# The last batch of an attention-and-Hyena kernel: output projection over four banks in the order in which its operand comes, own output buffers, final products on VectorE

## The chip, the cores and the metric

One core of a Trainium2 chip. The metric is the time of one execution in device microseconds (us), less is better. The kernel before takes 407.2 us (median of 4 runs, 406.5 to 408.2).

A second measure does much of the work here, because the change touches the last tenth of the program alone: the **stretch from batch 7's first eo to the end**, read from one trace as the span minus the start of the first of the two records that make tile eo (the even and odd halves of a batch, made in front of x2p) of the last batch. On every engine the changed kernel's order of instructions is that of the kernel before until this record. "After eo" below always means this.

## The reference

```python
def _attn_ref(q, k, v, omega):            # q, k, v: 8 batches, 8 heads, 576 rows, 64 columns
    ...                                   # random features cos, sin; kv = phi(k)^T v; num / den
x = attn_out.transpose(0, 2, 1, 3).reshape(8, 576, 512)
proj = x @ w_proj                         # 512 -> 3 x 512
x1, x2, x3 = proj[..., :512], proj[..., 512:1024], proj[..., 1024:]
x2_conv = irfft(rfft(x2, axis=1) * H)     # along the 576 rows
y = x1 * x2_conv * x3
out = y @ w_out                           # fp32, 8 x 576 x 512
```

## The kernel before

The batches go round a software pipeline: while one batch's attention part runs, the part after it (`hyena`) of the batch before runs beside it. In the last round there is only `hyena` of batch 7. A batch's `hyena` makes x2p (x2 before the transform), the spectrum (yp, ym, tc, yg), the gates (xg, w: x1 times x3), the inverse (xc, od, cv), the product yT, and the projection op with its copies o and their stores.

```python
        self.pt = self.pool("pt", 2, space=psum)          # two tiles of two PSUM banks, used by attention
        self.ps = self.pool("ps", 4, space=psum)          # four tiles of one bank, for everything else
...
    def inverse(self, b, dc):                              # 128 of the 512 columns
        ...                                                # xc on TensorE, od on ScalarE, cv on VectorE (bufs=2)
        nc.gpsimd.tensor_tensor(
            self.yT[b][:, dc], self.w.pop((b, dc)).rearrange("p a s -> p (a s)"),
            cv.rearrange("p c z i -> p (c z i)"), ALU.mult,
        )

    def project_out(self, b):
        nc, mo, yT = self.nc, self.mo, self.yT[b]
        every4 = self.out[b].rearrange("(i r) d -> r i d", r=4)
        for c in range(NC):                                # five chunks of 128, 128, 128, 128, 64 rows
            n = CH[c]
            ps = self.bank([128, DM], f"op{b}_{c}")
            _mm_acc(nc, ps[:n], [(yT[:, kc, 128 * c : 128 * c + n], self.wo[kc]) for kc in range(4)])
            o = mo.tile([128, DM], FP32, name=f"o{b}_{c}", tag="osb", bufs=2)
            nc.scalar.mul(o[:n], ps[:n], 1.0 / YS)
            for blk, i, m, at in _pieces(128 * c, n, QB):  # one or two stores a chunk, eight in all
                nc.sync.dma_start(every4[BLOCKS[blk], i : i + m], o[at : at + m])
...
        for b in range(B + 1):
            for hp in range(4):
                if b < B:
                    self.pair(b, hp)                       # attention
                ...
                if b:
                    self.hyena(b - 1, hp)
...
    def hyena(self, b, part):
        if part == 0:
            self.x2_project(b)
            self.gates(b, 0)
        elif part == 1:
            self.spectrum(b)
            self.gates(b, 1)
        elif part == 2:
            self.gates(b, 2)
            self.inverse(b, 0)
            self.gates(b, 3)
            self.inverse(b, 1)
        else:
            self.inverse(b, 2)
            self.inverse(b, 3)
            self.project_out(b)
```

Of the kernel before, what the change touches and what calls it, by code (L numbers as in the profile page):

```python
# [9 lines left out]
FP32 = mybir.dt.float32  # L10
# [5 lines left out]
ALU = mybir.AluOpType  # L16

B = 8
# [3 lines left out]
DM = H * D  # L22
NC = 5
CH = [128, 128, 128, 128, 64]
# [3 lines left out]
YS = 4096.0  # L28
# [6 lines left out]
QB = S // 4  # L35
EB = QB // 2
BLOCKS = [0, 1, 2, 3]
# [53 lines left out]
def _pieces(lo, n, block):  # L91

    at = lo
    while at < lo + n:
        k, i = divmod(at, block)
        m = min(block - i, lo + n - at)
        yield k, i, m, at - lo
        at += m
# [10 lines left out]
def _mm_acc(nc, outap, pairs):  # L109
    n = len(pairs)  # L110
    for i, (l, r) in enumerate(pairs):
        nc.tensor.matmul(outap, l, r, start=(i == 0), stop=(i == n - 1))  # L112
# [6 lines left out]
class _Program:  # L119
# [461 lines left out]
    def inverse(self, b, dc):  # L581
        nc, mo = self.nc, self.mo
        cols = slice(128 * dc, 128 * (dc + 1))
        if dc == 0:
            self.yT[b] = mo.tile([128, 4, S], FP16, name=f"yT{b}", tag="yT", bufs=1)
        half = []
        for g in (1, 0):
            ps = self.bank([128, HS], f"xc{b}_{dc}_{g}")
            ls = [self.yg[g][:, 0, cols], self.yg[g][:, 1, cols], self.ymix[:, cols]]
            _mm_acc(nc, ps, [(l, self.inv[:, 3 * g + i]) for i, l in enumerate(ls)])  # L590
            half.append(ps)
        od = mo.tile([128, HS], FP32, name=f"od{b}_{dc}", tag="od", bufs=2)
        nc.scalar.copy(od, half[0])
        cv = mo.tile([128, 4, 2, EB], FP32, name=f"cv{b}_{dc}", tag="cv", bufs=2)
        ev, ov = (x.rearrange("p (c i) -> p c i", i=EB) for x in (half[1], od))
        nc.vector.tensor_tensor(cv[:, :, 0], ev, ov, ALU.add)
        nc.vector.tensor_tensor(cv[:, :, 1], ev, ov, ALU.subtract)  # L597
        nc.gpsimd.tensor_tensor(  # L598
            self.yT[b][:, dc], self.w.pop((b, dc)).rearrange("p a s -> p (a s)"),
            cv.rearrange("p c z i -> p (c z i)"), ALU.mult,  # L600
        )

    def project_out(self, b):
        nc, mo, yT = self.nc, self.mo, self.yT[b]
        every4 = self.out[b].rearrange("(i r) d -> r i d", r=4)
        for c in range(NC):
            n = CH[c]
            ps = self.bank([128, DM], f"op{b}_{c}")
            _mm_acc(nc, ps[:n], [(yT[:, kc, 128 * c : 128 * c + n], self.wo[kc]) for kc in range(4)])
            o = mo.tile([128, DM], FP32, name=f"o{b}_{c}", tag="osb", bufs=2)  # L610
            nc.scalar.mul(o[:n], ps[:n], 1.0 / YS)  # L611
            for blk, i, m, at in _pieces(128 * c, n, QB):
                nc.sync.dma_start(every4[BLOCKS[blk], i : i + m], o[at : at + m])

    def run(self):
        for name in ("vf", "kT", "qT", "kf", "kft", "qf", "kvz", "xsd", "xT", "w", "yT", "marks", "pool_marks",
                     "first", "h"):
            setattr(self, name, {})
        self.pools()
        self.omega_load()  # L620
        self.first_loads()
        self.buffers()
        self.front(0, 0)
        self.second_loads()
        self.v_loads(1)
        self.weights()
        self.v_split_tails(0)
        for b in range(B + 1):
            for hp in range(4):
                if b < B:  # L630
                    self.pair(b, hp)
                if b == hp == 1:
                    self.filter_spectrum(1)
                    self.filter_spectrum(2)
                if b:
                    self.hyena(b - 1, hp)
                if b < 2:
                    self.opening(b, hp)

    def opening(self, b, hp):  # L640

        at = 4 * b + hp
        if at == 2:
            self.first_k_tails(1)
            self.first_k(1, 0)
        elif at == 3:
            self.first_k(1, 1)
            self.first_q(1, 3, 3)
        elif at == 4:
            with self.tc.issue_after(self.pool_marks["k", 1, 1].ins):  # L650
                self.loads(2)
            self.fold_filter()
            self.first_k(1, 2)
            self.first_q(1, 6, 2)
            self.filter_spectrum(0)
        elif at == 5:
            self.first_k(1, 3)
            self.out_weights()
# [27 lines left out]
# [12 lines that stand above are left out]
        else:  # L698
            self.inverse(b, 2)
            self.inverse(b, 3)  # L700
            self.project_out(b)



@with_exitstack
# [44 lines left out]
```

## Time and profile before

| | before |
|---|---|
| median of 4 runs, us | 407.17 |
| span of the profiled run, us | 404.8 |
| first eo of batch 7 to the end, us | 42.82 |
| yp starts, after eo | 14.40 |
| last yT ends, after eo | 31.47 |
| first copy o starts, after eo | 31.96 |
| last store issued, after eo | 39.38 |

The lines behind it are in the prediction: the chain of work that ended last, and the timeline, in which the brackets give the idle time of the engine before the instruction and what ended it.

### The profile page before, as it was taken

Reading aid. Unit: us, or ns where it says so; the run is one execution under the profiler, and the core shown is the slowest. Engines: PE = TensorE matmul, PEld = TensorE weight load, DVE = VectorE, ACT = ScalarE, POOL = GpSimd, SP = SyncE. Lnnn points to the kernel's source line nnn. Section 1 sums busy time; section 2 is a strip of 40 time slices with the busy share of each in tenths; the row PEclk is TensorE's granted clock in tenths of the full one; section 3 lists DMA queues with packets and bytes.
Section 4 is the critical chain, followed back from the end, with each engine's and each line's share of the span. In section 5 each row is a group of like instructions: output and inputs, shape, how many; then the busy total and the mean of one; then the engine's idle time right before and its main releaser. Section 6 shows DMA issues by size and latency. Waiting matters only on the chain.

```text
span 404.8 us, 9053 instructions
## 1 busy us (share of the span) xinstructions
PE 333.9 (82%) x3714; PEld 220.8 (55%) x3714; DVE 268.8 (66%) x489; ACT 246.1 (61%) x332; POOL 240.0 (59%) x222
## 2 busy tenths in 40 slices
PE   3786888987779978898789888997989888987981
PEld 2565645565336754566455744674557545663650
DVE  4686644777637887597839784978578784871740
ACT  1777766476675477746883679458764787124332
POOL 0654588669733977297827883597537672532450
PEclk9869589999889999999999999999999999999997
DMA  7999899636931593049613972369400021002103
GB/s 183 302 293 245 197 165 189 134 105 75 180 112 62 88 195 115 15 112 150 157 54 105 126 174 66 105 76 161 118 3 0 2 84 36 2 2 87 30 2 117
DMA packets 71465, 44.76 MB, mean 111 GB/s; under 512 B 38656, under 2 KB 64896, under 8 KB 71424
## 3 DMA queue, kind: packets, MB, share of 16 engines
q1 hardware_dynamic: 53712, 34.12, 33.2%
q0 software_dynamic: 17712, 10.06, 18.4%
q8 instruction: 29, 0.48, 0.5%
q14 instruction: 12, 0.10, 0.1%
HBM read 36.83 MB, written 16.52 MB: 132 GB/s over the span
## 4 chain that ended last, share of the span: by engine, by line
PE 34%; DVE 24%; POOL 17%; ACT 13%; issue 6%; DMA 4%; SPq 2%; POOLq 0%; ACTq 0%; DVEq 0%
PE xg L112 9%; PE kv L495 8%; DVE tc L559 7%; POOL yT L598 6%; ACT qf L479 5%; POOL angq L421 4%; DVE angk L420 4%; PE op L112 4%; PE nd L512 3%; PE xc L112 3%; DMA out_dram<-o 3%; PE x2p L112 3%; DVE angq L420 3%; ACT kf L458 3%; DVE xsd L518 2%
## 5 line engine op out<-in xcount | busy, mean ns | idle before, releaser
L458 ACT ACTIVATE kf<-angk 128x2048 f16<-128x2048 int16 x32 | 61.1, 1909 | 42.1 <-PE nd L512 18.0
L479 ACT ACTIVATE qf<-angq 128x1728 f16<-128x1728 int16 (+1 forms) x48 | 70.5, 1480 | 22.9 <-POOL angq L421 16.6
L112 PE MATMUL xg<-xT,wp 128*128 128x288 f16 x512 | 71.9, 286 | 1.3 <-ACT x L548 0.4
L420 DVE TENSOR_SCALAR angq<-thq 128x864 int32<-128x864 f32 (+1 forms) x48 | 45.7, 954 | 27.6 <-ACT qf L479 20.8
L112 PEld LDWEIGHTS <-wp 128*128 128x128 f16 x512 | 48.6, 97 | 20.8 <-issue 4.6
L401 POOL TENSOR_TENSOR vl<-vf,vh 128x512 f16<-128x512 f32 x32 | 39.1, 1221 | 31.6 <-ACT vh L400 31.2
L421 POOL TENSOR_SCALAR angk<-angk 128x1024 int32<-128x1024 int32 x32 | 33.5, 1047 | 34.7 <-DVE angk L420 33.7
L598 POOL TENSOR_TENSOR yT<-w,cv 128x576 f16<-128x576 f32 x32 | 45.1, 1430 | 14.5 <-DVE cv L597 7.4
L112 PE MATMUL op<-wo,yT 128*128 128x512 f16 (+1 forms) x160 | 42.7, 393 | 11.7 <-POOL yT L598 11.3
L421 POOL TENSOR_SCALAR angq<-angq 128x864 int32<-128x864 int32 (+1 forms) x48 | 43.1, 898 | 15.4 <-DVE angq L420 14.9
L578 DVE TENSOR_TENSOR w<-xg,w 128x288 f32<-128x288 f32 x64 | 27.4, 452 | 37.0 <-ACT w L576 19.3
L495 PEld LDWEIGHTS <-kf 128*128 128x128 f16 x1024 | 44.4, 101 | 13.1 <-issue 11.1
L560 POOL TENSOR_TENSOR yg<-tc,tc 128x1024 fp32r<-128x1024 f32 x16 | 37.4, 2359 | 23.6 <-DVE tc L559 22.1
L420 DVE TENSOR_SCALAR angk<-thk 128x1024 int32<-128x1024 f32 x32 | 39.0, 1219 | 16.7 <-PE thk L452 7.1
L576 ACT ACTIVATE w<-xg 128x288 f32<-128x288 f32 x64 | 24.5, 407 | 36.5 <-PE xg L112 35.8
L495 PE MATMUL kv<-vh,kf 128*128 128x65 f16 x512 | 39.1, 200 | 5.4 <-ACT w L576 4.7
L112 PE MATMUL x2p<-wp,eo 128*128 128x512 f16 x160 | 39.4, 403 | 2.8 <-DVE xsd L518 2.1
L559 DVE TENSOR_TENSOR tc<-yp,h 128x1024 f32<-128x1024 f32 x32 | 36.9, 1215 | 2.3 <-ACT vh L400 2.2
L495 PE MATMUL kv<-vl,kf 128*128 128x64 f16 x512 | 38.0, 198 | 0.2 <-POOL vl L401 0.2
L512 PE MATMUL nd<-kvz,qf 128*128 128x65 f16 x640 | 27.3, 197 | 10.3 <-DVE kvz L500 6.4
L611 ACT ACTIVATE o<-op 128x512 f32<-128x512 f32 (+1 forms) x40 | 22.9, 592 | 18.9 <-PE op L112 10.0
L512 PEld LDWEIGHTS <-qf 128*128 128x128 f16 x640 | 24.8, 99 | 16.2 <-issue 13.0
(84 smaller groups left out, 604.7 us busy)
## 6 DMA issues: line engine op xcount, KB each, us to landing
vf<-in_v_dram SPq DMA_DIRECT2D x7, 1024.0 KB, 5.4
qD<-in_q_dram POOLq DMA_DIRECT2D x6, 576.0 KB, 7.4
kD<-in_k_dram POOLq DMA_DIRECT2D x6, 512.0 KB, 5.8
ka<-in_k_dram SPq DMA_DIRECT2D x4, 512.0 KB, 11.4
out_dram<-o SPq DMA_DIRECT2D x8, 256.0 KB, 2.6
out_dram<-o SPq DMA_DIRECT2D x8, 224.0 KB
wp<-in_moe_w_proj_dram POOLq DMA_DIRECT2D x1, 1536.0 KB, 15.7
out_dram<-o SPq DMA_DIRECT2D x8, 192.0 KB
```

Of the source, the lines that this page charges most:

```text
L112: nc.tensor.matmul(outap, l, r, start=(i == 0), stop=(i == n - 1))
L401: nc.gpsimd.tensor_tensor(self.vl[hp], vp, vh, ALU.subtract)
L420: self.nc.vector.tensor_scalar(into, th, TO_PHASE, None, ALU.mult)
L421: self.pool_mark = self.nc.gpsimd.tensor_scalar(t[:, 1], t[:, 0], 1.0, TURN / 4, ALU.mult, ALU.add)
L458: self.marks["k", b, hp] = nc.scalar.activation(kf.rearrange("p t r a c m -> p t (r a c m)"), ang, AF.Sin, scale=TO_ANGLE)
L479: nc.scalar.activation(self.qf[b][:, :, a0 : a0 + n].rearrange("p t a r i -> p t (a r i)"), ang, AF.Sin, scale=TO_ANGLE)
L495: nc.tensor.matmul(ps[:, hh, t, : 1 + D] if i < 5 else ps[:, hh, t, :D], l, r_, start=(i == 0), stop=(i == len(terms) - 1),)
L512: nc.tensor.matmul(ps[:, c], qfh[:, t, SOFF[c] : SOFF[c] + 128], kvz[:, hh, t], start=(t == 0), stop=(t == 1),)
L559: nc.vector.tensor_tensor(t[i], ps[:, None, :].broadcast_to([128, 2, DM]), hc, ALU.mult)
L560: nc.gpsimd.tensor_tensor(self.yg[g], t[0], t[1], ALU.add)
L578: nc.vector.tensor_tensor(w[:, ns], ps, w[:, ns], ALU.mult)
L598: nc.gpsimd.tensor_tensor(self.yT[b][:, dc], self.w.pop((b, dc)).rearrange("p a s -> p (a s)"), cv.rearrange("p c z i -> p (c z i)"), ALU. ...
```

## The change

Its intent: with no other batch left to fill waits, the last batch is to end sooner. x2p of batch 7 goes ahead of batch 6's projection; all gates ahead of all inverses; the last two yT products to VectorE; op accumulates all five chunks at once in banks that attention no longer needs, one round for each quarter of yT as it comes; each output copy has a buffer of its own; copies alternate between ScalarE and VectorE.

```diff
-        nc.gpsimd.tensor_tensor(
+        eng = nc.vector if b == B - 1 and dc > 1 else nc.gpsimd
+        eng.tensor_tensor(
             self.yT[b][:, dc], ...
+    def project_out_last(self, b):
+        nc, yT = self.nc, self.yT[b]
+        two = [self.pt.tile([128, 2, DM], FP32, name=f"op{b}_{i}", tag="th") for i in range(2)]
+        ps = [two[c // 2][:, c % 2] for c in range(4)] + [self.bank([128, DM], f"op{b}_4")]
+        for kc in range(4):
+            for c in range(NC):
+                n = CH[c]
+                nc.tensor.matmul(
+                    ps[c][:n], yT[:, kc, 128 * c : 128 * c + n], self.wo[kc], start=(kc == 0), stop=(kc == 3)
+                )
+        for c in range(NC):
+            n = CH[c]
+            tag = ("tc0", "tc1", "tc0", "tc1", "osb")[c]
+            o = self.mo.tile([128, DM], FP32, name=f"o{b}_{c}", tag=tag, bufs=2)
+            if c % 2:
+                nc.vector.tensor_scalar(o[:n], ps[c][:n], 1.0 / YS, None, ALU.mult)
+            else:
+                nc.scalar.mul(o[:n], ps[c][:n], 1.0 / YS)
+            self.store(b, c, o)
...
-        for b in range(B + 1):
+        for b in range(B):
...
+        self.closing(B - 1)
...                                          # hyena, part 3:
-            self.project_out(b)
+            if b < B - 2:
+                self.project_out(b)
...
+    def closing(self, b):
+        self.x2_project(b)
+        self.project_out(b - 1)
+        self.gates(b, 0)
+        self.spectrum(b)
+        for dc in range(1, 4):
+            self.gates(b, dc)
+        for dc in range(4):
+            self.inverse(b, dc)
+        self.project_out_last(b)
```

More of the change, by code (lines that the diff above doesn't have):

```diff
@@ L603, in project_out @@
     def project_out(self, b):
-        nc, mo, yT = self.nc, self.mo, self.yT[b]
-        every4 = self.out[b].rearrange("(i r) d -> r i d", r=4)
         for c in range(NC):
@@ L608, in project_out, with store @@
             ps = self.bank([128, DM], f"op{b}_{c}")
-            _mm_acc(nc, ps[:n], [(yT[:, kc, 128 * c : 128 * c + n], self.wo[kc]) for kc in range(4)])
-            o = mo.tile([128, DM], FP32, name=f"o{b}_{c}", tag="osb", bufs=2)
-            nc.scalar.mul(o[:n], ps[:n], 1.0 / YS)
-            for blk, i, m, at in _pieces(128 * c, n, QB):
-                nc.sync.dma_start(every4[BLOCKS[blk], i : i + m], o[at : at + m])
+            _mm_acc(self.nc, ps[:n], [(self.yT[b][:, kc, 128 * c : 128 * c + n], self.wo[kc]) for kc in range(4)])
+            o = self.mo.tile([128, DM], FP32, name=f"o{b}_{c}", tag="osb", bufs=2)
+            self.nc.scalar.mul(o[:n], ps[:n], 1.0 / YS)
+            self.store(b, c, o)
+    def store(self, b, c, o):
+        every4 = self.out[b].rearrange("(i r) d -> r i d", r=4)
+        for blk, i, m, at in _pieces(128 * c, CH[c], QB):
+            self.nc.sync.dma_start(every4[BLOCKS[blk], i : i + m], o[at : at + m])
+    def project_out_last(self, b):
[16 more added lines that the diff above has]
+                nc.scalar.mul(o[:n], ps[c][:n], 1.0 / YS)
+            self.store(b, c, o)
     def run(self):
@@ L627, in run @@
         self.v_split_tails(0)
-        for b in range(B + 1):
+        for b in range(B):
             for hp in range(4):
-                if b < B:
-                    self.pair(b, hp)
+                self.pair(b, hp)
                 if b == hp == 1:
```

## The prediction

> **What bounds the kernel now.** I read the list of cores first (one core, 404.8 us, granted clock 0.955), then the chain that ended last in order of time from 340 us on, then the timeline of all engines from 358 us on, then the changed kernel's order of instructions and waits against the old one's. That order is the same on every engine until batch 7's even and odd halves (tile eo) are made. So only what follows 361.9 us can change: 43 us, in which one batch is left and nothing of another batch can fill a wait.
>
> The chain of the kernel before, its last part (start, length, what):
>
> ```profile
> 366.84 2.45 PE op L112 x10
> 369.29 0.98 PE x2p L112 x4
> ...
> 374.54 1.96 PE xg L112 x16
> 376.50 0.66 PE yp L112 x3
> 377.19 3.50 DVE tc L559 x3
> ...
> 388.38 0.46 DVE cv L596
> 388.83 0.37 DVE cv L597
> 389.21 0.07 issue
> 389.28 2.77 POOL yT L598 x2
> 392.05 1.37 POOLq L745
> 393.42 0.05 issue
> 393.47 0.40 PE op L112
> 393.87 0.02 issue
> 393.89 0.60 ACT o L611
> 394.51 2.46 DMA out_dram<-o
> ```
>
> The reader is to see three stretches. (1) The projection op of batch 6 stands ahead of x2p of batch 7 on TensorE, and waits for GpSimd's yT. (2) GpSimd's yT products end the chain of batch 7 at 393.4. (3) Then come copies (ACT o) with a landing of 2.46 us between them; the chain goes on with two more of the same.
>
> The timeline of the same kernel shows the waits of stretch 1 and 3:
>
> ```profile
> 362.90 1.47 PE L112 MATMUL op<-wo,yT 128*128 128x512 f16 x6
> 364.97 1.04 PE L112 MATMUL op<-wo,yT 128*128 128x512 f16 x4 [0.59 <-POOL yT L598]
> 366.84 2.45 PE L112 MATMUL op<-wo,yT 128*128 128x512 f16 x10 [0.83 <-POOL yT L598]
> 397.08 0.60 ACT L611 ACTIVATE o<-op 128x512 f32<-128x512 f32 x1 [2.10 <-DMA out_dram<-o]
> 400.70 0.59 ACT L611 ACTIVATE o<-op 64x512 f32<-64x512 f32 x1 [2.18 <-DMA out_dram<-o]
> ```
>
> ScalarE is idle for 2.10 and 2.18 us because the output tile has two buffers: the third and fifth copy wait for a store of the first and third to land. From the last yT (393.41) to the end (404.75) it takes 11.3 us, of which copies take 2.9.
>
> **What the Trainium skill says.** "DMA: Bandwidth & Descriptors", section "Anatomy of one DMA", gives a fixed cost of about 2 us per DMA, most of it the receipt of the write; it states it for the gpsimd path, but the stores here, from SyncE, agree: 2.4 to 2.5 us from issue to the copy that it releases. "VectorE: DVE Perf Modes", section "The TRN2 errata", gives (N+151)/0.96 ns for an fp32 tensor_tensor: 757 ns at N=576. The trace has 1215 ns at N=1024 (formula 1224) and 450 at 288 (457), so it agrees. "PSUM — Partial Sum Buffer", section "PSUM bank collisions raise a hardware error", wants accesses of two engines to one bank kept apart. In the built program the wait is coarser: the new op tile of two banks is one tile, and VectorE's copy of its second bank waits for ScalarE's copy of its first. No run shows yet what that costs. "SBUF — State Buffer", section "Who interferes with whom", says a VectorE operation with two SBUF inputs and a GpSimd operation that reads SBUF block one another. The trace agrees: eo takes 0.76 us alone at 361.94, 1.45 us beside yT at 364.07, and that yT takes 1.91 instead of 1.40.
>
> **The change part by part.** Durations are the old trace's: a group of four 512-column matmuls 0.863 us plus 0.17 until its result is readable; four 288-column ones 0.49; an xc group 0.40; copies 0.59 (512 columns) and 0.40 (288); a tc product every 1.13; hand-over between engines 0.05. I place each instruction at the latest of its waits in the built program.
>
> (a) x2p before op of batch 6. Its first two groups need only the first eo (362.69): they run 362.90 to 364.63. The other three need the second eo, whose place and time are unchanged (365.52): 365.58 to 368.17. The yT of batch 6 is done at 366.78 by then, so op no longer waits: 368.2 to 372.5. Removed are waits of 0.6 and 0.8 us; it still idles 0.95 for eo. The new order lets batch 6's stores touch the path: the o copies 3 and 5 wait for landings (o copy 1 ends 369.85, landed 372.3; copy 2's two stores 373.6; copy 3's 375.9), and the next banks wait for the copies. xg of the first gate runs 372.5 to 374.7; yp needs the bank of o copy 4, which ends at 374.7. So yp starts at about 374.75 instead of 376.34: **1.6 us gained**. The fifth copy ends at 376.5, when the fourth yp group wants its bank at 376.7: just in time.
>
> (b) All gates before all inverses. The same matmuls; from yp's start to the last xc 13.53 us go by in the old trace. The sum of the pieces is 12 and 5 at 0.216, 12 xg groups at 0.49, 8 xc groups at 0.40 = 12.75. I find waits of 0.35 (for tc and the w products) where the old order has 0.78. Last xc readable at 388.0, before 389.87: with (a) **1.9 us**. GpSimd gets its first product later relative to this (cv ready 386.5, so 386.6 to 388.0, the second to 389.35).
>
> (c) The last two products on VectorE. VectorE's order is cv2, cv2, cv3, yT2, cv3, yT3, and cv3 takes a buffer that GpSimd's second product frees at 389.35. So cv3 runs at 389.40, yT2 389.8 to 390.5, cv3's second half to 390.9, yT3 waits for it and ends at 391.7. Before, 393.41: with (a) and (b) **1.7 us**. The faster engine buys little beyond the earlier start, because the buffer wait puts it behind GpSimd; GpSimd alone would have ended at 392.1 (four products at 1.37 from 386.6).
>
> (d) Four banks free and kc outermost: before, 12 matmuls remained after the last yT (2.88 us), now five (five at 0.216 = 1.1). But they only set the first copy: op of chunk 0 and 1 is readable 0.6 after 391.75, so 392.4; before 0.42 after. **No gain by itself**, it lets the copies come at once.
>
> (e) Own output buffers, copies on two engines. Removed: the two landings in front of copies 3 and 5. ScalarE copies chunk 0 from 392.4 to 393.0, VectorE chunk 1 (0.69 us, from 1219 ns at 1024 columns) to 393.7, ScalarE chunks 2 and 4 to 394.0, VectorE chunk 3 to 394.3. Now SyncE's issuing leads: eight stores, each occupying its queue 0.37 (first of a pair) to 0.52 us (second) in the old trace. Chunk 1's first store starts at 393.75; from it .39+.53+.37+.52+.43+.50 = 2.74 us to the last store, 396.5. In the old trace the last store's issue to its landing takes 2.27 us and the landing to the end 1.16. End 396.5 + 3.43 = 399.9. From last yT to end: 8.2 us instead of 11.3, **3.1 us gained**.
>
> Sum: 1.6 + 0.3 - 0.2 + 3.1 = 4.8 us (the -0.2 is the chain from xc to last yT, 3.7 instead of 3.5). Span 400.0; time 407.48 - 4.8 = **402.7 us**, 1.2% less.
>
> **The rivals.** R1: batch 6's stores become the wait. With x2p ahead, nothing covers the landings that its copies 3 to 5 wait for; were they 1 us longer than I place them, yp would start 1 us later. For it: the chain of bank, copy and landing has no slack in my placing. Against: 2.45 us is seen throughout. It would leave a gain of 3.0 to 4.0: 403.5 to 404.5 us. R2: issue is not the bound at the end but the store transfers. Two chunks of batch 7 moved in 2.1 us in the old trace, so 4.5 chunks want at most 4.7 from about 393.9: 398.6 for the last byte, and with the 0.4 us from last byte to release that the old end shows 399.0, against 398.8 in mine; time 403. R3: VectorE's new products run freely beside GpSimd and its copy doesn't wait, so the tail shrinks to one landing and pipelined copies, yT at 391 and stores well spread: a gain of 7 to 8 us, 399.5 to 400.5. The waits of the built program and the eight issues of 3.2 us in total speak against it; this is the only way near 2%, which needs 8.15 us. R4: nothing before 393 is gained, since the start of the spectrum is bound elsewhere (eo, GpSimd's yT of batch 6, or SyncE): only 3.1 stays, 404.4.
>
> **Range and chances.** Each placing can be off by some 0.3 us, and R1 and R4 draw upward, R3 downward; the three runs of before lie 1.7 us apart, so the median alone can move by 0.5. I take 400.7 to 404.6. Faster by over 2% needs all of R3: 0.05. Slower by over 2% would need a new stall of 13 us, and nothing moved is longer than a landing: 0.01. The rest, 0.94, is within 2%.
>
> **What would show it.** Step (a): x2p at 362.9 and yp near 374.75, with ACT o waiting for landings twice in between. If yp starts after 375.7, R1 holds; if batch 7's x2p is no earlier, R4. Step (b): the last xc near 388. Step (c): VectorE's two yT of about 0.75 us each, the first right after the cv that waits for GpSimd, the last ending near 391.7. Step (e): no wait of ACT o for a landing at the end, SyncE's eight issues back to back for some 3.5 us, the last near 396.5. If they have gaps, copies lead, not issues; if the last landing comes over 2.6 us after its issue, R2. From the last yT to the end 8.2 us. I am wrong if the time falls below 400.7 or stays above 404.6.

## The result, and the profile after

The changed kernel takes 403.0 us (median of 4 runs, 401.8 to 403.9). The ratio is 0.9894, 95% interval 0.986 to 0.9927: 1.1% less, within 2%. (Ratios here are the mean time of one kernel's fast runs over that of the other's of the same rounds, so not quite the ratio of the medians quoted.) In the profiled runs the stretch after eo falls from 42.82 to 39.05 us, by 3.77; the median falls by 4.2, of which 0.4 lies in the part that did not change, or in chance.

The chain that ended last in the changed kernel, its last part (start, length, what):

```profile
387.25 1.44 POOL yT L599
388.69 0.05 issue
388.74 4.59 PE op L626 x17
...
393.41 0.61 ACT o L636
394.02 0.02 issue
394.04 0.69 DVE o L634
394.73 0.60 DVEq L780
```

No landing stands between the copies any more. But what was the wait for the last yT is now 4.59 us of TensorE's op itself.

The timeline of the changed kernel, the lines that answer to those of before:

```profile
363.24 1.90 PE L112 MATMUL x2p<-wp,eo 128*128 128x512 f16 x8
365.92 2.76 PE L112 MATMUL x2p<-wp,eo 128*128 128x512 f16 x12 [0.79 <-DVE eo L540]
368.52 4.60 PE L112 MATMUL op<-wo,yT 128*128 128x512 f16 x20
372.60 0.60 ACT L610 ACTIVATE o<-op 128x512 f32<-128x512 f32 x1 [1.55 <-DMA out_dram<-o]
375.25 2.75 PE L112 MATMUL yp<-x,fwd 128*128 128x512 f16 x12
388.74 5.34 PE L626 MATMUL op<-wo,yT 128*128 128x512 f16 x20 [0.18 <-POOL yT L599]
390.08 0.46 DVE L596 TENSOR_TENSOR cv<-xc,od 128x288 f32<-128x288 f32 x1 [0.54 <-POOL yT L599]
390.45 0.75 DVE L599 TENSOR_TENSOR yT<-w,cv 128x576 f16<-128x576 f32 x1
391.60 0.76 DVE L599 TENSOR_TENSOR yT<-w,cv 128x576 f16<-128x576 f32 x1
394.04 4.35 SPq L616 DMA_DIRECT2D out_dram<-o  x8
```

Batch 6's op (20 matmuls) no longer waits for yT. Batch 7's op takes 5.34 us for 20 matmuls, where 20 at 0.216 us and one latency would be 4.5. The last yT ends at 392.36, but the last round of op starts only at 392.70, after the third. The view of waits from 389 us on says what stands in front of the weight loads (PEld): who waited for what, us in total, times, longest:

```profile
PEld L626 <- issue: 1.5, 4, 0.4
```

Four waits in which nothing that the profile shows was waited for. The single records of the trace show where: after a matmul with 128 columns of weights the next one follows by 0.216 us, but chunk 4's (64 columns) follows by 0.31 and the one after it by 0.34. (In the first round it follows by 0.40, because it also waits for GpSimd's second yT, which ends 27.77 us after eo; the matmul starts at 27.83. In x3 and z4 below, where that yT is there before, it is 0.34 in every round.) Chunk 4's weights are loaded after most of a pause, and the next weights only when chunk 4's matmul has all but ended.

### The profile page after: what moved, and what is told of

Read it like the earlier page. It is cut to its first block, busy times and chain, and to the rows that moved or that the text cites. A ratio compares the mean times of both kernels' runs of the same rounds, so it can differ in the third digit from the quotient of the medians.

```text
span 401.3 us, 9049 instructions
## 1 busy us (share of the span) xinstructions
PE 334.1 (83%) x3714; PEld 220.8 (55%) x3714; DVE 271.6 (68%) x493; ACT 245.4 (61%) x330; POOL 236.9 (59%) x220
## 4 chain that ended last, share of the span: by engine, by line
PE 35%; DVE 24%; POOL 16%; ACT 13%; issue 6%; DMA 3%; SPq 1%; DVEq 0%; ACTq 0%; POOLq 0%
PE xg L112 9%; PE kv L495 8%; DVE tc L559 7%; ACT qf L479 6%; POOL angq L421 5%; POOL yT L599 5%; DVE angk L420 4%; PE op L112 4%; PE nd L512 3%; ACT kf L458 3%; DVE angq L420 3%; PE xc L112 3%; DVE xsd L518 2%; POOL vl L401 2%; PE x2p L112 2%
## 5 line engine op out<-in xcount | busy, mean ns | idle before, releaser
L599 POOL TENSOR_TENSOR yT<-w,cv 128x576 f16<-128x576 f32 x30 | 42.4, 1431 | 15.1 <-DVE cv L597 10.2
L112 PE MATMUL op<-wo,yT 128*128 128x512 f16 (+1 forms) x140 | 37.3, 394 | 8.8 <-POOL yT L599 8.3
L518 DVE TENSOR_TENSOR xsd<-nd,rd 128x320 f16<-128x320 f32 x64 | 30.0, 485 | 0.7
```

The costliest lines, as they stand in the source:

```text
L112: nc.tensor.matmul(outap, l, r, start=(i == 0), stop=(i == n - 1))
L518: nc.vector.tensor_tensor(xsd[:, :, D * hh : D * hh + D], ps[:, :, :D], rden[:, :, None].broadcast_to([128, NC, D]), ALU.mult,)
L599: eng.tensor_tensor(self.yT[b][:, dc], self.w.pop((b, dc)).rearrange("p a s -> p (a s)"), cv.rearrange("p c z i -> p (c z i)"), ALU.mult,)
```

## The experiments

The kernels "only" start from the kernel before; the others from the changed one, unless said. Times in the table are us after eo. Medians are of 6 runs each, and each ratio compares with 11 runs of the kernel before in the same rounds (medians 406.43 for x, 406.79 for y, 406.52 for z); in the first two lines they are of the 4 runs of the result. All results were correct.

| kernel | yp starts | last yT ends | first copy | first store's first byte | last issue | end | median | ratio (95%) |
|---|---|---|---|---|---|---|---|---|
| before | 14.40 | 31.47 | 31.96 | 33.43 | 39.38 | 42.82 | 407.17 | |
| changed | 12.98 | 30.09 | 31.14 | 32.61 | 35.62 | 39.05 | 403.0 | 0.9894 (0.986-0.9927) |
| x1 buffers only | 14.41 | 31.45 | 31.99 | 33.46 | 36.24 | 39.66 | 403.51 | 0.9921 (0.9892-0.9951) |
| x2 x2p first only | 12.97 | 30.04 | 30.52 | 31.99 | 37.86 | 41.28 | 404.82 | 0.996 (0.9923-0.9997) |
| x3 new tail only | 14.40 | 31.06 | 32.38 | 33.86 | 36.85 | 40.26 | 404.61 | 0.995 (0.9915-0.9986) |
| x4 GpSimd products | 12.98 | 30.51 | 31.26 | 32.74 | 35.74 | 39.32 | 402.66 | 0.9902 (0.9869-0.9935) |
| y1 chunk 4 last | 12.98 | 30.09 | 30.85 | 32.32 | 35.31 | 38.73 | 402.34 | 0.9891 (0.9871-0.9912) |
| y2 chunk 4 wide | 12.98 | 30.10 | 30.86 | 32.33 | 35.34 | 38.78 | 403.0 | 0.9898 (0.9874-0.9923) |
| y3 tile per engine | 12.98 | 30.09 | 31.14 | 32.61 | 35.40 | 38.99 | 403.41 | 0.9919 (0.9892-0.9946) |
| y4 two queues | 12.98 | 30.10 | 31.15 | 32.62 | 33.81 | 38.94 | 402.45 | 0.9898 (0.9874-0.9923) |
| z1 buffers and x2p only | 12.98 | 30.02 | 30.56 | 32.03 | 34.81 | 38.23 | 401.91 | 0.9882 (0.9857-0.9906) |
| z2 = z1, VectorE products | 12.98 | 29.64 | 30.31 | 31.78 | 34.57 | 38.01 | 402.62 | 0.9887 (0.9863-0.991) |
| z3 old op and copies | 12.97 | 30.09 | 30.77 | 32.24 | 35.03 | 38.45 | 402.38 | 0.9894 (0.9873-0.9916) |
| z4 old gate order | 12.97 | 29.63 | 30.94 | 32.41 | 35.42 | 38.85 | 402.69 | 0.9902 (0.9873-0.9931) |

The whole times can't tell most of these versions apart: their intervals are 1.7 to 3 us wide (only x2 and x3 have intervals apart from those of z1, z2 and y1). The stretch can. One trace stands behind each figure of it; its repeatability is the agreement of the columns where kernels share code, so a difference of under some 0.15 us in the end is not safe.

### Theory and rivals

Theory: the gain is x2p's 1.4 to 1.6 us and the removed landings' 3 us; the rest brings nothing or costs. Rivals: the reorder or the banks carry the gain. And for what ends the tail now: the issuing of the stores, or their transfers.

### x1: own output buffers only

```diff
-            o = mo.tile([128, DM], FP32, name=f"o{b}_{c}", tag="osb", bufs=2)
+            tag = ("tc0", "tc1", "tc0", "tc1", "osb")[c] if b == B - 1 else "osb"
+            o = mo.tile([128, DM], FP32, name=f"o{b}_{c}", tag=tag, bufs=2)
```

> The kernel before with one part of the change: the last batch's output copies get buffers of their own, nothing else. If the removed landings make most of the gain, as the sum of the prediction has it: no wait of ACT o for a landing at the end, SyncE's eight issues back to back from 394.5, and the stretch from batch 7's first eo to the end (42.8 us before, 39.0 with the whole change) shrinks by 3.2 to 3.6 us, to 39.2 to 39.6: nearly the whole gain. Rival: the reorder of x2p and the bank order carry it; then less than 2 us come from the buffers.

The stretch shrank by 3.16 us, to 39.66. The timeline of this run, and its chain, have no landing between copies; all eight stores are issued in one go:

```profile
394.21 4.11 SPq L614 DMA_DIRECT2D out_dram<-o  x8
```

```profile
393.10 2.90 PE op L112 x12
396.00 0.02 issue
396.02 0.59 ACT o L612
```

A buffer for each of the five o tiles, in place of two for all, is thus worth 3.16 us, where the whole change gains 3.77. The theory stands, this rival falls.

### x2: x2p first only

```diff
         if part == 0:
-            self.x2_project(b)
+            if b < B - 1:
+                self.x2_project(b)
...
             self.inverse(b, 3)
+            if b == B - 2:
+                self.x2_project(b + 1)
             self.project_out(b)
```

> The kernel before with x2p of batch 7 ahead of op of batch 6, nothing else. Step (a): yp starts 12.95 to 13.0 us after the first eo (14.4 before), and as the later chain is the old one, the whole stretch shrinks by 1.2 to 1.5 us, to about 41.4. Rival: GpSimd's products or the landings of batch 6 take it back before the end; then the stretch shrinks by less than 0.5.

yp starts at 12.97 and the stretch is 41.28: 1.54 us less (1.2 to 1.5 expected). But 3.16 and 1.54 make 4.7, more than the whole change's 3.77. So the other parts together must cost about 0.9 us, unless these two overlap.

### x3: the new tail only

The edit: the changed kernel with `closing` and `hyena` putting x2p, gates, inverses and batch 6's projection in the order of the kernel before.

> The new tail (four banks, outermost kc, own buffers, VectorE's products and copies) in the old order of everything before it. If bank order, VectorE's products and VectorE's copies buy nothing of their own: no better than own buffers alone, 39.5 to 40.2 us from eo to end, rather worse by up to 0.7, since VectorE's copy waits for ScalarE's and TensorE loses time at each change between 128 and 64 columns of weights. Rival: they are worth something, then it is below 39.2.

40.26: 0.60 worse than own buffers alone, within the "up to 0.7" that was expected, and a little over the range of 39.5 to 40.2. The last yT came 0.39 us sooner than in x1, and the first copy 0.39 later. VectorE's products do bring something, and the op in rounds takes more than it back.

### x4: products on GpSimd

```diff
-        eng = nc.vector if b == B - 1 and dc > 1 else nc.gpsimd
+        eng = nc.gpsimd
```

> The changed kernel with all four products of the last batch on GpSimd again. TensorE, not the product, sets the fourth round of op in the changed kernel (it starts 0.34 us after the last yT ends): GpSimd's last product should end near 0.4 later, and the stretch to the end grow by 0.1 to 0.3 us only. Rival: the products on VectorE are what ends the chain sooner, then it grows by 0.7 or more.

The last yT ended 0.42 us later, the first copy started 0.12 later, the end came 0.27 later: inside what was expected. A part of what VectorE gains is lost, since TensorE is late for it; the stores then took 0.14 us longer from first byte to end, as the last one landed 2.40 us after its issue (2.26 in the changed kernel), which is not explained.

### y1 and y2: what the pauses in op are

y1:

```diff
-        for kc in range(4):
-            for c in range(NC):
+        for kc, c in [(kc, c) for kc in range(4) for c in range(4)] + [(kc, 4) for kc in range(4)]:
```

> The changed kernel with chunk 4's four matmuls (64 columns of weights) after all others instead of one in each round. In the changed kernel each change of width costs: 0.31 us from matmul to matmul into it and 0.33 to 0.40 out of it, against 0.216. Taken out of the rounds, the last round starts as soon as the last yT is there and the first copy 0.3 to 0.4 us sooner; the stretch from eo to the end shrinks by 0.3 to 0.4 us. Rival: issue of stores alone sets the end, then nothing changes.

y2 (chunk 4's weights are rows 448 to 575 of yT, so its result stands in partitions 64 to 127):

```diff
-                n = CH[c]
-                nc.tensor.matmul(ps[c][:n], yT[:, kc, 128 * c : 128 * c + n], ...)
+                lo = min(128 * c, S - 128)
+                nc.tensor.matmul(ps[c], yT[:, kc, lo : lo + 128], ...)
...
+            r = slice(128 - n, 128)            # the copies and the store read o[r], ps[c][r]
```

> The changed kernel with chunk 4 computed with 128 columns of weights (its own 64 and the 64 before them, whose result is not used), still once in each round. If the width is what costs, all matmuls of op stand 0.216 us apart and the first copy comes 0.3 to 0.4 us sooner. If the change of bank or the order of weights costs, the gaps of 0.31 to 0.40 stay.

Both bring the first copy 0.28 to 0.29 us sooner (0.3 to 0.4 expected) and shrink the stretch by 0.32 and 0.27. The group of op's matmuls by source line shows what TensorE and its weight loads sat idle for (us, times). In the changed kernel:

```profile
L626 PE MATMUL op<-wo,yT x20: 379/379/403, 388.7 to 393.7; 128*128 128x512 f16 x16, 128*64 128x512 f16 x4
...
  issue: 1.5, 4
  POOL yT L599: 0.9, 3
```

In y2:

```profile
L626 PE MATMUL op<-wo,yT x20: 379/379/390, 389.4 to 394.0; 128*128 128x512 f16 x20
...
  POOL yT L599: 1.2, 3
  DVE yT L599: 0.8, 2
```

With one width the four "issue" pauses are gone, though order and banks are the same; what is left is waiting for yT. So the change of width between 128 and 64 columns is what costs. The weight loads themselves took 95 to 106 ns at both widths. The Trainium skill has a mechanism that fits: "TensorEngine Tiling (Array Packing)", section "Tiling Modes", says that changing the tiling mode drains TensorE, and lists 128x64 beside 128x128 as modes. It gives no time, and that a drain is the cause is not shown beyond the weight loads' waiting. Here one chunk in each round cost 0.09 us going in and 0.12 coming out, over the regular 0.216; the 0.40 of the two expectations above has a wait for yT in it. The kernel before goes into it once, since chunk 4's four matmuls stand together.

### y3: each tile copied by one engine

```diff
-        ps = [two[c // 2][:, c % 2] for c in range(4)] + ...
+        ps = [two[c % 2][:, c // 2] for c in range(4)] + ...
...
-            for c in range(NC):                # matmuls
+            for c in (0, 2, 1, 3, 4):
```

> The changed kernel with chunks 0 and 2 in one two-bank tile and 1 and 3 in the other, so that each tile is copied by one engine and VectorE's copy no longer waits for ScalarE's. VectorE starts 0.4 us after ScalarE instead of 0.63, SyncE's second store 0.2 us sooner, and the end 0.2 us sooner. Rival: the wait costs more than that, because the copies are on the path all the way: 0.5 us or more.

VectorE's first copy started 0.26 us sooner (31.51), all later stores were issued 0.21 to 0.26 sooner, and the end came 0.06 sooner. Half of the expectation failed: the issue moved, the end hardly. One trace doesn't settle why. x1, z1, z2 and z3 issue their eight stores in the same rhythm (the last 3.62 to 3.64 us after the first), and their end comes 7.04 to 7.07 us after the first issue; here it came after 7.23, because the last store landed 2.42 us after its issue instead of 2.26.

### y4: two queues

```diff
-            self.nc.sync.dma_start(...)
+            eng = self.nc.scalar if b == B - 1 and c in (2, 4) else self.nc.sync
+            eng.dma_start(...)
```

> The changed kernel with the last batch's stores of chunks 2 and 4 issued by ScalarE, the others by SyncE. If issuing bounds the end: last issue near 1.8 us sooner and the end 1.8 us sooner. If the transfers bound it (rival R2): the stores' packets keep the DMA engines busy for 3.8 us from 394.9 on, so the last byte can come only 1.0 to 1.1 us sooner, however early it is issued.

The last store was issued 1.81 us sooner, the end came 0.11 us sooner. The stores' first byte went at the same time after eo (32.62 against 32.61), the last only 0.28 sooner (37.24 against 37.52). So the expectation missed under either reading: the end was to come 1.8 us sooner, or the last byte 1.0 to 1.1. The view by stretches, over the time of the stores' packets: after the colon-separated stretch and its length come the engines, then PE clock, DMA share of all 16 engines, GB/s. The changed kernel, then y4:

```profile
394.80:399.80 5.00, 0.00 (x0) 0.00 (x0) 0.53 (x1) 0.17 (x1) 0.00 (x0) 0.67 0.76 238
```

```profile
393.40:398.10 4.70, 0.00 (x0) 0.00 (x0) 0.53 (x1) 0.16 (x1) 0.00 (x0) 0.82 0.85 251
```

The DMA engines move the batch's 1.18 MB at 238 and 251 GB/s. Issuing far sooner only packs them a little tighter. That is what "DMA: Bandwidth & Descriptors", section "Issuing engines are not separate DMA queues", says of a second issuing engine: it saves the sequencer's time alone. So from the first byte the end follows after 6.2 to 6.6 us, in every kernel without landings between copies: 6.20 in x1, 6.44 in the changed kernel, 6.58 in x4, 6.32 in y4. The time of the first byte is what counts most.

That does not take the issuing off the path where one queue issues all. The landing records of the traces show it: in the kernel before and in x2 the last store is issued alone, long after the others, and lands 2.26 us after its issue; the end comes 1.18 and 1.16 us after that. In the changed kernel it is the same 2.26 and 1.17, and 2.25 to 2.27 in all one-queue kernels but x4 and y3. So the last store did not wait for other transfers, and its issue leads to the end. But the lead is small. In y4 the stores do wait for one another (the last one issued lands 3.78 us after its issue), and the last landing comes only 0.29 us sooner (37.59 against 37.88 after eo). Of this the end gets 0.11, mostly because SyncE's wait for the last landing ends 0.16 us after it there, and 0.01 to 0.02 after it elsewhere. Issuing and transfers are thus two paths that end within 0.3 us of each other.

### z1 to z4: do the paying parts add up, and what do the others cost

z1 has both edits of x1 and x2. z2 has also the first line of the change (VectorE for dc > 1). z3 is the changed kernel with `project_out` (with x1's tags) in place of `project_out_last`. z4 is the changed kernel with the gates and inverses of `closing` in the old order:

```diff
-        for dc in range(1, 4):
-            self.gates(b, dc)
-        for dc in range(4):
-            self.inverse(b, dc)
+        self.gates(b, 1)
+        self.gates(b, 2)
+        self.inverse(b, 0)
+        self.gates(b, 3)
+        for dc in range(1, 4):
+            self.inverse(b, dc)
```

> The kernel before with the two parts that paid alone (own output buffers for the last batch, x2p of the last batch ahead of op of the batch before), and nothing of the rest: old order of gates, products on GpSimd, op and its copies as they were. Alone they took 3.16 and 1.54 us off the stretch from eo to the end. If they add up, it is 38.1 us, 0.9 less than the whole change's 39.05, and the rest of the change costs time. If they overlap, it is 39.0 or more.

> As z1, and the last two products of the last batch on VectorE. In the tail-only run, which had the old order of gates, the last yT came 0.4 us sooner than with GpSimd's products. If that carries over: 37.7 us from eo to end, the best of all. If in the old order the products are not on the path: as z1.

> The changed kernel with the last op and its copies as for every other batch (banks of the common pool, each chunk's four matmuls as banks allow, all copies on ScalarE), but with own buffers. If four banks and copies on two engines cost more than they bring: from the last yT to the end 8.2 us as in the buffers-only run instead of 9.0, so 38.3 us from eo to the end. Rival: they bring something, then it is 39.1 or more.

> The changed kernel with the old order of gates and inverses in the last batch. If computing all gates first brought nothing and took VectorE's products their 0.4 us: last yT at 29.6 to 29.7 instead of 30.1 us after eo, and 38.6 to 38.8 to the end. If the gates-first order brought the 0.3 us that the prediction gave it: 39.3 or more.

z1 came to 38.23 (38.1 if they added up): they do, nearly, and z1, with two small edits, has a stretch 0.82 us shorter than the whole change. z2 came to 38.01, 0.22 less; 0.4 was expected, and the last yT did come 0.38 sooner, but the first copy only 0.25. z3 came to 38.45 (38.3 expected), z4 to 38.85 (38.6 to 38.8). They make a ladder from before to the changed kernel, one part at a time (each step is a difference of the column "end"):

| step | us |
|---|---|
| before to x2: x2p first | -1.54 |
| x2 to z1: own output buffers | -3.05 |
| z1 to z2: last two products on VectorE | -0.22 |
| z2 to z3: all gates before all inverses | +0.44 |
| z3 to changed: op in rounds, two tiles of two banks, copies on two engines | +0.60 |
| sum | -3.77 |

Why the gates-first order costs, the timelines say. VectorE's cv lines with a wait for GpSimd's yT, in z2, whose eo starts at 364.25:

```profile
390.16 1.41 POOL L599 TENSOR_TENSOR yT<-w,cv 128x576 f16<-128x576 f32 x1 [1.27 <-DVE cv L597]
390.49 0.45 DVE L597 TENSOR_TENSOR cv<-xc,od 128x288 f32<-128x288 f32 x1
391.60 0.46 DVE L596 TENSOR_TENSOR cv<-xc,od 128x288 f32<-128x288 f32 x1 [0.66 <-POOL yT L599]
391.97 0.75 DVE L599 TENSOR_TENSOR yT<-w,cv 128x576 f16<-128x576 f32 x1
```

The last cv waits for GpSimd's second product in both orders, since it takes that product's buffer. In z2 this wait ends 27.35 us after eo (391.60), in the changed kernel 27.81 (390.08 less 362.27). With all gates first, GpSimd has its first product only after them, and its second right behind; in the old order the first is done while TensorE works on the last gate. The last xc comes 0.2 sooner for it and the last yT 0.45 later.

Of the 0.60, y1 shows 0.32 to be the change of width. Most of the rest, 0.20 of 0.28, shows behind the first byte: from there to the end it is 6.41 us in y1 (6.44 in the changed kernel) and 6.21 in z3. In the changed kernel the second store is issued 0.73 us behind the first, since VectorE waits for ScalarE and then takes 0.69 us; with ScalarE alone 0.49. From the last issue to the end it is 3.42 to 3.44 us in all of these, so the later row of issues accounts for it. But that closing the gap would win it back is not shown: y3 closed most of the gap and won 0.06, with a last landing that was 0.16 us slow.

By the stretch z2 is the best version that was run. By whole times the best median is z1's, 401.91 (ratio 0.9882); neither is told from the changed kernel by its interval.

## Why the prediction was right or wrong

The time was predicted as 402.7 us and is 403.0; the stretch was to fall by 4.8 and fell by 3.77. That the time came so close is in part luck: the stretch gained 1.03 us less than forecast, but 0.4 came from outside it, and the median before was 407.17, not the 407.48 that the sum started from. One reading was loose: after the landing of 2.46 us the chain goes on with one more landing (2.48), not with "two more of the same"; the sum has two. Step by step:

- **Step (a)**, x2p first, 1.6 us. Measured: yp 1.42 sooner in the changed kernel, the end 1.54 sooner where it stands alone. Right (yp 12.98 after eo, where the step has 12.8). The landings of batch 6 are waited for by its copies, for 1.55 and 0.80 us, but yp begins right at the end of the four gate groups in front of it, so rival R1 falls. R4 falls too.
- **Step (b)**, all gates first, 0.3 us at the last xc, taken off again by 0.2 in (c). Measured: 0.2 sooner at the last xc, but 0.46 later at the last yT (changed against z4) and 0.20 to 0.44 at the end. The step saw that the first product comes later but put the price too low, since it did not work out what VectorE's products would do in the old order.
- **Step (c)**, little from VectorE's products because of the buffer wait. Right as to the wait and nearly as to the time: last yT 30.09 after eo where the step has 29.8. They took 0.75 and 0.76 us, where the formula that the prediction cites gives 0.757. They bring 0.42 at the last yT and 0.22 to 0.27 at the end.
- **Step (d)** failed: "now five (five at 0.216 = 1.1)". The changes of width make a round 1.30 us (start of the second round to the third, 390.10 to 391.40) instead of 1.08, so the third round was not over when the last yT came. This term is 0.3 us larger than the step has it, shown by y1 and y2; "No gain by itself" was in fact a loss.
- **Step (e)**: own buffers alone bring the 3.1 us (3.16 and 3.05), so the second copying engine added nothing. In the changed kernel itself the time from the last yT to the end fell by 2.4, from 11.35 to 8.96 us, where the step has 8.2. Its mechanism, "Now SyncE's issuing leads", held as far as the runs show: the last landing is 2.26 us after the last issue and the end 1.17 after that, where the step has 2.27 and 1.16. The sign that the prediction set for rival **R2**, a last landing over 2.6 us after its issue, did not appear. But R2 is close behind: it put the bytes of the five chunks at at most 4.7 us; the changed kernel has 4.91, y4, with the issuing out of the way, 4.62, and its last landing is just 0.29 us sooner. What the step sized wrong is the row of issues: 4.48 us from the first copy to the last issue, where it has 4.1.
- **R3** falls: the waits of VectorE's copy were there as the built program has them.

So the excess of 1.09 us in the end of the stretch (39.05 against the predicted 399.9 - 361.94 = 37.96) is 0.33 in the last yT, 0.35 more until the first copy, mostly the width, and 0.41 in the stores, most of it in front of the eighth. What stays open is why the eighth store of a row on SyncE's queue starts 0.35 us later than the pattern of the seven before gives it (35.62 after eo, not 35.27); SyncE issued nothing for 0.44 or 0.45 us in front of it in all eleven kernels that issue eight in a row, though its copy had long ended. With two queues no store has such a gap before it.

## What to carry to other kernels

When the end of a program is one batch's copy and store, count its buffers first: a buffer for each output tile took away two landings, 3 us here, while more banks and more engines for the same copies brought nothing, and a second queue 0.1 us: the issuing that it takes away leads by little, and the transfers are right behind it. In a loop over accumulators keep matmuls of one weight width together, or give the narrow one the width of the others. Judge a change to a stretch by that stretch in the trace, measured from a record that both kernels share: the whole time drifts by more than the parts are worth.

## What the Trainium skill lacked or had wrong

- "TensorEngine Tiling (Array Packing)" says that a change of mode drains TensorE, but not what it costs, nor that a chunk of 64 columns of weights among chunks of 128 is such a change: 0.31 us into it and 0.34 out of it, against 0.216 between equal ones.
- "DMA: Bandwidth & Descriptors" gives its fixed cost of about 2 us for the gpsimd path. For stores from SyncE no page that I read gives the time; the runs show 2.4 to 2.5 us from issue to the copy that waits for it, for 128 rows of 2 KB, and 2.26 us from issue to landing for a lone one of 64 rows. For eight such stores in a row, 1.18 MB, they show 238 to 251 GB/s, in packets of 2 KB.
- No page that I read explains why the eighth store in a row on one queue starts 0.35 us late with its data ready; the cause is not shown here either.
- "PSUM — Partial Sum Buffer" has collisions by bank and quadrant. A tile of two banks was guarded as one in the built program, though its banks are apart: VectorE's copy waited for ScalarE's. Freed from that wait (y3), its copy began 0.26 us sooner and the end came 0.06 us sooner.
